# An attention and feed-forward kernel: its planner keeps VectorE's and GpSimd's port work apart, with new planned durations

## The chip, the cores and the metric

The kernel runs on one core of a Trainium2 chip. The metric is device time in microseconds (us). A core has five engines with instruction queues of their own: TensorE (PE; its weight loads are PEld), VectorE (DVE), ScalarE (ACT), GpSimd (POOL) and SyncE (SP), which here issues all DMAs. Engines wait for one another through semaphores only.

## The reference

```python
scores = 1/sqrt(D) * q @ k.T                      # B, H, S, D = 4, 8, 576, 64
psi_rel = log1p(|i - j|); psi_i = log1p(max(i, 1))
bias = relu((psi_rel / psi_i) * w1 + b1) @ w2     # 32 hidden units, one bias per head
attn = softmax(scores + bias)                     # sum + 1e-9 in the divisor
x = (attn @ v) laid out as (B*S, H*D)             # 2304 x 512
h = x @ w_in                                      # 512 x 2048
out = (h * sigmoid(h)) @ w_out                    # 2048 x 512
```

The weights w_in and w_out are 64-bit floats in DRAM; everything else is float32.

## The kernel before, in words

Every step is an operation of a plan: a kind, the engines that may run it with a planned duration for each, a due time, the tiles it reads and writes. `Plan.order` (L118) plays the plan: whenever an engine is free in it, it starts the ready operation with the earliest due time (with a penalty for an engine that is slow for it, not on GpSimd), until all are placed. The result is nothing but one fixed row of instructions per engine; on the chip each engine runs its row in order and waits by semaphores for what it reads. So a planned duration never makes anything wait on the chip: it decides which engine gets an operation, and behind what.

Three parts follow one another and overlap at their seams.

First, the bias (`bias_tile`, L311): 36 tiles, each with four `bias_f` (L326 ScalarE, L328 VectorE or GpSimd), a matmul (L334) and an eviction (L341, L343), written to DRAM and read back as slabs. Beside it runs the attention of batch 0.

Attention (`chunk`, L537; `visit`, L463): keys and queries are split into a float32r part and a remainder (`k_hi`, `k_lo`, `q_hi`, `q_lo`; the casts are L270 on ScalarE and L272 on VectorE, the subtractions L275 on GpSimd or VectorE). Then score matmuls (`s_mm` L561, `s_last` L552), the maximum with the bias (L568, VectorE, scores read from PSUM), the exponential (L575, ScalarE), transposes (L584), evictions (L270, L272) and the product with v (L483). Four head pairs per batch, five chunks of rows each; the row sums go through `sum` and `recip` (L515, L519).

Feed-forward (`ff_block`, L659; `ff_step`, L627): six blocks of 384 tokens, 16 steps each. A block's x is scaled and split (`split_x`, L599: `x_mul` L614, `x_hi`, `x_lo`), a step is 12 matmuls of `h_mm` (L633), tanh (L638), the gate (L642), a split of its result (`g_hi`, `g_lo`) and 9 matmuls of `out_mm` (L656), due two steps after. In block 0, while the attention of batches 1 and 2 runs, each of 32 weight tiles is first brought from 64-bit to 32-bit floats (`narrow`, L349: `abs` L356 on ScalarE, then `clamp` L360, `shift` L364, `low` L369, `sign` L374 on VectorE) and split by `prepare` (L377: `split_hi` on ScalarE, `split_lo` on GpSimd or VectorE, both L270 and L275). The split w_in goes to DRAM and is read again by the later blocks.

TensorE fills gaps of the first 24 us with warm-up matmuls on a zero tile (L723), placed where the plan has it idle.

Of the kernel before, what the change touches and what calls it, by code (L numbers as in the profile page):

```python
# [46 lines left out]
class Plan:  # L47
# [11 lines left out]
    LAG = {"PE": 0.2, "ACT": 0.15, "DVE": 0.13, "POOL": 0.15, "SP": 0.95}  # L59
# [58 lines left out]
    def order(self):  # L118
        ops = self.ops
# [12 lines left out]
        num, dma, mode = 0, 0.0, 0  # L132
# [13 lines left out]
        while events:  # L146
# [17 lines left out]
            for e in sorted(free, key=lambda e: free[e]):  # L164
# [8 lines left out]
                while wait[e]:  # L173
# [42 lines left out]
def attention_moe_kernel(ctx: ExitStack, tc: tile.TileContext, q, k, v, small, w_in, w_out, lut, ident_d, out):  # L216
# [94 lines left out]
    def bias_tile(st, t0):  # L311
# [8 lines left out]
        for ig in range(4):  # L320
            @op("bias_f", {"ACT": 0.22 + n * 0.00086, "DVE": 0.15 + n * 0.0009} if ig or st % 2 == 0 or st < 4 else {"POOL": 0.12 + n * 0.0045},
# [27 lines left out]
    def narrow(t0, w, src):  # L349
# [17 lines left out]
        @op("low", ("DVE", 0.9), t0 + 0.3, reads=[d], writes=[w])  # L367
# [35 lines left out]
    def keys(b, hp, t0):  # L403
# [8 lines left out]
        for a in range(2):  # L412
            @op("k_lo", {"POOL": 1.55, "DVE": 0.95}, t0 - 6 + 0.1 * a, reads=[kst, khi], writes=[(klo, a)])
# [10 lines left out]
    def queries(b, hp, chunks, t0):  # L424
# [6 lines left out]
        @op("q_hi", {"ACT": 0.2 + 0.00083 * w, "DVE": 0.1 + 0.00056 * w}, t0 - 5, reads=[qst], writes=[qs])  # L431
# [3 lines left out]
        @op("q_lo", {"POOL": 0.12 + 0.0025 * w, "DVE": 0.1 + 0.0014 * w}, t0 - 4, reads=[qst], writes=[qs])  # L435
# [6 lines left out]
    def bias_of(hp, c, t0):  # L442
# [6 lines left out]
        if last:  # L449
            @op("bias_pad", ("POOL", 0.4), t0 - 9.1, writes=[bias])  # L450
# [51 lines left out]
    def sums(t0):  # L502
# [3 lines left out]
        @op("sq_zero", ("POOL", 0.3), t0 - 3, writes=[sq])  # L506
# [4 lines left out]
    def factors(b, hp, sq, t0):  # L511

        @op("sum", {"DVE": 0.17, "POOL": 0.3}, t0 + 4, reads=[(sq, i) for i in range(9)], writes=[sq])
# [3 lines left out]
        @op("recip", ("DVE", 0.2), t0 + 4.1, writes=[sq])  # L517
# [19 lines left out]
    def chunk(b, hp, c, i, x0, d0, khi, klo, qs, pt, sm, sq, t0):  # L537
# [27 lines left out]
        for a in range(heads):  # L565
            @op("max", ("DVE", 0.23 + width * 0.00105), t0 + 0.5 + 0.5 * a, reads=[sps[a], bias], writes=[(p, a), (sm, i + a)])
# [221 lines left out]
```

## Time and profile before

| | |
|---|---|
| time, median of 3 runs | 736.9 us (735.35 to 737.13) |
| profiled execution: span | 734.3 us |
| PE matmul busy | 712.6 us, 97% of the span |
| DVE busy | 421.0 us, 57%, 862 instructions |
| ACT busy | 389.4 us, 53%, 820 instructions |
| POOL busy | 281.4 us, 38%, 277 instructions |
| DMA | 154.77 MB, mean 211 GB/s |

The page gives no other time of the profiled execution than its span; the runs' times include what lies around it. Busy shares are averages over stages: DVE's busy tenths stand at 9 through most of the first 45% of the span and at 1 to 2 in the last third. "PE busy" counts matmuls whose ends are modelled, so a full PE isn't PE at its peak; the rate of matmuls has to be read from a stretch in which they follow one another.

### The profile page before, as it was taken

The page shows a single profiled execution, that of the slowest core. Times are in us where ns is not written, and L with a number is a line of the kernel's source. Part 1 is how long each engine was busy: PE and PEld are TensorE (multiplying, and loading weights), DVE is VectorE, ACT ScalarE, POOL GpSimd, SP SyncE. Part 2 cuts the span into 40 slices and gives each one's busy share as a digit, 9 for nine tenths or more (in the row PEclk, how much of TensorE's full clock was granted, in tenths as well). Part 3 has the DMA queues.
Part 4 walks back from the last instruction along what each step waited for, and adds up shares of the span by engine and source line. Part 5 has one row for each costly group of instructions (what it writes and reads, how often), then busy time and mean ns, then how long its engine had stood idle before and what let it go on. Part 6 is the DMA issues. An engine that isn't in the chain of part 4 may idle for free.

```text
span 734.3 us, 13019 instructions
## 1 busy us (share of the span) xinstructions
PE 712.6 (97%) x4642; PEld 590.1 (80%) x4642; DVE 421.0 (57%) x862; ACT 389.4 (53%) x820; POOL 281.4 (38%) x277
## 2 busy tenths in 40 slices
PE   9899999999999999989999999999999999999997
PEld 4376698677777787778888888899998999999996
DVE  6999968999999999996553544213211221211111
ACT  8899968886786777765443454222222232222222
POOL 5464524474746445573122251123223322422221
PEclk9999999999999999999999999999999999999999
DMA  6998899898584594879856567736454644346001
GB/s 195 372 315 270 277 310 359 278 289 297 191 290 157 203 303 149 272 257 311 293 165 224 168 217 241 263 115 196 148 162 153 186 150 152 125 136 195 1 0 44
DMA packets 68384, 154.77 MB, mean 211 GB/s; under 512 B 9056, under 2 KB 24032, under 8 KB 68320
## 3 DMA queue, kind: packets, MB, share of 16 engines
q1 hardware_dynamic: 68320, 153.94, 63.7%
q8 instruction: 37, 0.61, 0.4%
q14 instruction: 27, 0.22, 0.1%
HBM read 125.12 MB, written 28.79 MB: 210 GB/s over the span
## 4 chain that ended last, share of the span: by engine, by line
PE 46%; issue 7%; DVE 3%; POOL 2%; DMA 1%; ACT 0%; POOLq 0%; DVEq 0%; ACTq 0%
PE psum L633 18%; PE psum L656 18%; PE psum L483 3%; PE psum L561 3%; PE psum L584 3%; POOL M L275 2%; DVE G L568 1%; DVE w L369 1%; DMA G<-in_k_dram 1%; PE psum L552 1%; DVE M L275 0%; DVE w L374 0%; DVE th L642 0%; DVE M L272 0%; DVE w L360 0%
## 5 line engine op out<-in xcount | busy, mean ns | idle before, releaser
L633 PE MATMUL psum<-M,G 128*128 128x384 f32 x1152 | 238.8, 339 | 1.0 <-POOL M L275 0.8
L656 PE MATMUL psum<-G,M 128*128 128x512 f32 x864 | 238.0, 397 | 1.2 <-DVE M L275 0.9
L633 PEld LDWEIGHTS psum<-M,G 128*128 128x128 f32 x1152 | 203.4, 188 | 16.6 <-POOL M L275 1.0
L275 POOL TENSOR_TENSOR M<-th,M 128x384 fp32r<-128x384 f32 x82 | 84.9, 1035 | 272.0 <-ACT M L270 189.3
L642 DVE SCALAR_TENSOR_TENSOR th<-th,psum 128x384 f32<-128x384 f32 x96 | 53.0, 552 | 216.4 <-ACT th L638 216.4
L656 PEld LDWEIGHTS psum<-G,M 128*128 128x128 f32 x864 | 156.7, 188 | 22.2 <-DVE M L275 1.6
L575 ACT ACTIVATE G<-G,sm 128x576 f32<-128x576 f32 (+1 forms) x144 | 111.8, 777 | 53.6 <-DVE sm L568 52.3
L638 ACT ACTIVATE th<-psum 128x384 f32<-128x384 f32 x96 | 47.1, 491 | 161.1 <-PE psum L633 160.0
L568 DVE CUSTOM_DVE_ANT_0 G<-psum,G 128x576 f32<-128x576 f32 (+1 forms) x144 | 106.5, 758 | 27.9 <-PE psum L561 15.5
L584 PE MATMUL psum<-ident,G 128*128 128x128 f32 x656 | 93.5, 276 | 5.7 <-DVE sm L568 3.3
L561 PE MATMUL psum<-G,M 128*128 128x288 f32 x512 | 90.9, 310 | 4.9 <-DVE sm L568 3.5
L584 PEld LDWEIGHTS psum<-ident,G 128*128 128x128 f32 x656 | 75.3, 141 | 23.0 <-issue 4.8
L561 PEld LDWEIGHTS psum<-G,M 128*128 128x128 f32 x512 | 73.9, 190 | 19.7 <-issue 6.7
L483 PE MATMUL psum<-pt,M 128*64 128x128 f32 (+3 forms) x880 | 87.5, 346 | 1.6 <-DVE sm L568 0.8
L483 PEld LDWEIGHTS psum<-pt,M 128*64 128x64 f32 x880 | 52.1, 137 | 30.7 <-issue 6.8
L270 ACT ACTIVATE pt<-psum 128x512 f32<-128x512 f32 (+3 forms) x111 | 59.4, 551 | 28.1 <-PE psum L584 27.0
L275 POOL TENSOR_TENSOR M<-M 64x256 fp32r<-64x256 f32 (+3 forms) x40 | 48.6, 1217 | 57.9 <-DVE M L272 21.0
L270 ACT ACTIVATE M<-th 128x384 fp32r<-128x384 f32 x81 | 42.3, 523 | 40.9 <-DVE th L642 40.0
L272 DVE COPY pt<-psum 128x512 f32<-128x512 f32 (+3 forms) x81 | 45.4, 571 | 21.8 <-PE psum L584 19.1
L275 POOL TENSOR_TENSOR G<-w,G 128x512 fp32r<-128x512 f32 x25 | 35.6, 1425 | 23.8 <-ACT G L270 19.9
L275 POOL TENSOR_TENSOR G<-G 128x576 fp32r<-128x576 f32 x21 | 32.2, 1540 | 29.6 <-PE psum L334 9.6
L326 ACT ACTIVATE G<-lut_sb,cb 128x528 f32<-128x528 f32 (+16 forms) x71 | 41.6, 662 | 0.0
(55 smaller groups left out, 574.1 us busy)
## 6 DMA issues: line engine op xcount, KB each, us to landing
G<-win_d SPq DMA_DIRECT2D x80, 512.0 KB
G<-bias_d SPq DMA_DIRECT2D x48, 576.0 KB
bias_d<-G SPq DMA_DIRECT2D x36, 295.5 KB
G<-in_k_dram SPq DMA_DIRECT2D x16, 576.0 KB
G<-in_w_in_dram SPq DMA_DIRECT2D x16, 512.0 KB
G<-in_w_out_dram SPq DMA_DIRECT2D x16, 512.0 KB
win_d<-G SPq DMA_DIRECT2D x16, 512.0 KB
M<-in_v_dram SPq DMA_DIRECT2D x16, 320.0 KB
```

The source lines that it names most:

```text
L270: A.activation(out=out, in_=in_, func=AF.Copy)
L272: ENG[e].tensor_copy(out=out, in_=in_)
L275: ENG[e].tensor_tensor(out=out, in0=in0, in1=f(in1), op=ALU.subtract)
L483: T.matmul(out=tl(o)[x, 0:w], lhsT=tl(vs)[:, (s + 1) % 5 * 128 + 64 * a:(s + 1) % 5 * 128 + 64 * a + 64], rhs=tl(pt)[:, s + 5 * a if s < 4 ...
L561: T.matmul(out=s[:, hf, 0:288], lhsT=tl(qs)[:, x0 + 128 * a:x0 + 128 * a + 128], rhs=tl(part)[:, S * a + 288 * hf:S * a + 288 * hf + 288], ...
L568: V.tensor_tensor_reduce(out=mine(p, a).rearrange("p (a n) -> p a n", a=2), in0=tl(sps[a]).rearrange("p (a n) -> p a n", a=2)[:, :, 0:widt ...
L575: A.activation(out=mine(p, a), in_=mine(p, a), func=AF.Exp, scale=-1.0, bias=tl(sm)[:, i + a:i + a + 1], accum_out=tl(sq)[:, 2 * c + a:2 * ...
L584: T.transpose(out=tl(tp)[:, 128 * s:128 * s + 128], in_=tl(p)[:, 128 * (s0 + s):128 * (s0 + s) + 128], identity=ident)
L633: T.matmul(out=tl(hp)[:, 0:TB], lhsT=tl(wr)[:, x, 128 * cc:128 * cc + 128], rhs=tl(xs[cc])[:, y, :], start=(cc + m == 0), stop=(cc == NC - ...
L638: A.activation(out=tl(th), in_=tl(hp)[:, 0:TB], func=AF.Tanh, scale=0.5)
L642: V.scalar_tensor_tensor(out=tl(th), in0=tl(th), scalar=1.0, in1=tl(hp)[:, 0:TB], op0=ALU.add, op1=ALU.mult)
L656: T.matmul(out=tl(acc[i]), lhsT=tl(gg)[:, x, 128 * i:128 * i + 128], rhs=tl(wo[fi])[:, y, :], start=(fi == 0 and m == 0), stop=(fi == NF - ...
```

## The change

Three things in the planner, none in what is computed:

- Operations that are listed in `PORT`, per engine, share one resource in the plan: while one of them runs on VectorE or GpSimd, none of them is started on either. For VectorE these are the casts, splits, the narrowing, `bias_f` and `lut`; for GpSimd the two-input operations and `sum`. GpSimd's `bias_f` and memsets aren't in it.
- When several engines are free at the same time of the plan, GpSimd now chooses last.
- Planned durations and lags are new. Nothing changes in due times, buffer counts or stage constants.

```diff
-    LAG = {"PE": 0.2, "ACT": 0.15, "DVE": 0.13, "POOL": 0.15, "SP": 0.95}
+    LAG = {"PE": 0.18, "ACT": 0.14, "DVE": 0.12, "POOL": 0.1, "SP": 0.95}
+
+    PORT = {"DVE": {"lut", "bias_f", "clamp", "shift", "low", "sign", "split_lo", "k_hi", "k_lo", "q_hi", "q_lo", "x_mul", "x_hi", "x_lo", "g_hi", "g_lo"},
+            "POOL": {"split_lo", "k_lo", "q_lo", "x_mul", "x_lo", "g_lo", "sum"}}
...
-            for e in sorted(free, key=lambda e: free[e]):
+            for e in sorted(free, key=lambda e: (e == "POOL", free[e])):
...
-                    if not self.take(ops[i][4]):
+                    shared = self.kinds[i] in self.PORT.get(e, ())
+                    if shared and port > now or not self.take(ops[i][4]):
...
                     free[e] = end
+                    if shared:
+                        port = end
...
-        @op("clamp", ("DVE", 0.5), t0 + 0.1, writes=[w])
+        @op("clamp", ("DVE", 0.34), t0 + 0.1, writes=[w])
...
-        @op("low", ("DVE", 0.9), t0 + 0.3, reads=[d], writes=[w])
+        @op("low", ("DVE", 0.6), t0 + 0.3, reads=[d], writes=[w])
...
-        @op("split_lo", {"POOL": 1.36, "DVE": 0.9}, t0 + 1, reads=[w, (wr, 0)], writes=[(wr, 1)])
+        @op("split_lo", {"POOL": 1.24, "DVE": 0.6}, t0 + 1, reads=[w, (wr, 0)], writes=[(wr, 1)])
...
-            @op("max", ("DVE", 0.23 + width * 0.00105), t0 + 0.5 + 0.5 * a, reads=[sps[a], bias], writes=[(p, a), (sm, i + a)])
+            @op("max", ("DVE", 0.08 + width * 0.00116), t0 + 0.5 + 0.5 * a, reads=[sps[a], bias], writes=[(p, a), (sm, i + a)])
...
-        @op("g_lo", {"DVE": 0.55, "POOL": 1.1}, t0 + 2.6, reads=[th, (gg, 0)], writes=[(gg, 1)])
+        @op("g_lo", {"DVE": 0.47, "POOL": 0.96}, t0 + 2.6, reads=[th, (gg, 0)], writes=[(gg, 1)])
```

The other planned durations on VectorE, ScalarE and GpSimd go down in the same manner; those of TensorE and SyncE stay. All lines of the file behind the new ones are 6 higher (L275 becomes L281).

How the rows change. Over the whole program VectorE's row goes from 864 to 968 instructions, GpSimd's from 282 to 153, ScalarE's from 678 to 703; TensorE's differs by its warm-ups (82 before, 63 now). The subtraction of the gate's split (g_lo, `M<-th,M`) was on GpSimd 82 times of 96 and is there 7 times now.

GpSimd, a piece of its row in the middle of the weight narrowing (`G<-w,G` is split_lo, `M<-th,M` g_lo, `M<-M` q_lo, `G<-G` k_lo), before:

```order
L275 TENSOR_TENSOR G<-w,G 128x512
L275 TENSOR_TENSOR M<-M 64x512
L275 TENSOR_TENSOR G<-G 128x576 x2
L275 TENSOR_TENSOR G<-w,G 128x512
L275 TENSOR_TENSOR M<-th,M 128x384
L275 TENSOR_TENSOR G<-w,G 128x512
L275 TENSOR_TENSOR M<-M 64x704
L275 TENSOR_TENSOR G<-w,G 128x512
L275 TENSOR_TENSOR M<-th,M 128x384
```

and with the change:

```order
L281 TENSOR_TENSOR G<-G 128x576
L514 MEMSET sq 128x128
L281 TENSOR_TENSOR M<-M 64x512
L281 TENSOR_TENSOR G<-w,G 128x512
L281 TENSOR_TENSOR M<-M 64x704
L281 TENSOR_TENSOR G<-w,G 128x512
L281 TENSOR_TENSOR M<-th,M 128x384
L521 TENSOR_SCALAR sq<-sq 128x9
```

Between its first and last split_lo GpSimd had 71 two-input operations and has 42 now; the g_lo and part of each of the other kinds went to VectorE.

VectorE at the same place of the narrowing (L360 and L366 clamp, L364 and L370 shift, L369 and L375 low, L374 and L380 sign, `ISA G,sm<-psum,G` the maximum), before:

```order
L642 SCALAR_TENSOR_TENSOR th<-th,psum 128x384
L374 SCALAR_TENSOR_TENSOR w<-G,w 128x512
L364 TENSOR_SCALAR w<-w 128x512
L369 SCALAR_TENSOR_TENSOR w<-G,w 128x512
L275 TENSOR_TENSOR G<-w,G 128x512
L568 ISA G,sm<-psum,G 128x576
```

and with the change:

```order
L375 SCALAR_TENSOR_TENSOR w<-G,w 128x512
L380 SCALAR_TENSOR_TENSOR w<-G,w 128x512
L278 COPY pt<-psum 128x4x128
L366 TENSOR_SCALAR w<-w 128x512
L281 TENSOR_TENSOR G<-w,G 128x512
L370 TENSOR_SCALAR w<-w 128x512
L648 SCALAR_TENSOR_TENSOR th<-th,psum 128x384
```

The steps of the narrowing and the maxima stand there as often as before (32 tiles, 62 maxima between the first and the last step); what came in between them are subtractions.

VectorE at the end of its row, before (15 gates in a row, whose g_lo stand on GpSimd):

```order
L642 SCALAR_TENSOR_TENSOR th<-th,psum 128x384 x15
L683 TENSOR_SCALAR M<-psum 128x512
L683 TENSOR_SCALAR M<-psum 128x256
```

and with the change:

```order
L648 SCALAR_TENSOR_TENSOR th<-th,psum 128x384
L281 TENSOR_TENSOR M<-th,M 128x384
L648 SCALAR_TENSOR_TENSOR th<-th,psum 128x384
L281 TENSOR_TENSOR M<-th,M 128x384
L689 TENSOR_SCALAR M<-psum 128x512
L689 TENSOR_SCALAR M<-psum 128x256
```

Each gate is followed there by its own subtraction, which reads ScalarE's cast.

## Rows read from the trace of the kernel before

**Rows 1.** Busy time by stage; columns: stretch, its length, busy time (and instructions) by engine.

```profile
core 0: us, PE busy (x) PEld busy (x) DVE busy (x) ACT busy (x) POOL busy (x), PEclk, DMA share, GB/s
0.00:127.30 127.30, 122.58 (x1195) 84.25 (x1195) 107.50 (x256) 107.57 (x230) 60.94 (x72) 0.99 0.91 299
127.30:318.80 191.50, 179.78 (x1206) 144.91 (x1205) 185.35 (x342) 144.16 (x303) 102.23 (x89) 1.00 0.72 242
335.00:728.00 393.00, 393.00 (x2144) 346.57 (x2140) 113.36 (x235) 124.33 (x258) 107.47 (x108) 1.00 0.51 164
```

**Rows 2.** Chain of waits, 335 to 360 us; columns: start, length, what.

```profile
334.71 2.84 PE psum L483 x20
...
339.75 2.09 PE psum L633 x12
...
342.55 0.98 PE psum L584 x9
...
344.92 1.05 PE psum L561 x8
345.97 2.31 PE psum L483 x20
...
352.74 2.07 PE psum L656 x9
```

**Rows 3.** Groups of TensorE's matmuls, 127.3 to 318.8 us; columns as in the page's part 5.

```profile
L561 PE MATMUL psum<-G,M 128*128 128x288 f32 x223 | 40.4, 308 | 3.0 <-DVE sm L568 1.5 <-DVE pt L272 1.0 <-ACT pt L270 0.4
L483 PE MATMUL psum<-pt,M 128*64 128x256 f32 (+2 forms) x320 | 40.2, 398 | 1.6 <-DVE sm L568 0.8 <-DVE th L642 0.6
L584 PE MATMUL psum<-ident,G 128*128 128x128 f32 x287 | 40.1, 275 | 4.7 <-DVE sm L568 3.3 <-DVE pt L272 0.7 <-ACT pt L270 0.5
L633 PE MATMUL psum<-M,G 128*128 128x384 f32 x183 | 38.2, 345 | 1.0 <-POOL M L275 0.8
L656 PE MATMUL psum<-G,M 128*128 128x512 f32 x129 | 34.8, 399 | 0.9 <-DVE M L275 0.9
```

**Rows 4.** Timeline at 205 to 212 and 376 to 378 us; columns: start, length, instruction.

```profile
205.49 1.69 POOL L275 TENSOR_TENSOR M<-M 64x704 fp32r<-64x704 f32 x1 [3.89 <-issue]
205.54 1.92 DVE L360 TENSOR_SCALAR w<-w 128x512 f32<-128x512 f32 x1
...
209.07 0.68 DVE L369 SCALAR_TENSOR_TENSOR w<-G,w 128x512 uint32<-128x512 uint32 x1
209.67 0.55 DVE L275 TENSOR_TENSOR M<-th,M 128x384 fp32r<-128x384 f32 x1
...
211.42 0.42 DVE L360 TENSOR_SCALAR w<-w 128x512 f32<-128x512 f32 x1
...
377.02 0.75 DVE L275 TENSOR_TENSOR G<-G 128x576 fp32r<-128x576 f32 x1
```

**Rows 5.** Groups of VectorE's narrowing steps, 127.3 to 318.8 us.

```profile
L369 DVE SCALAR_TENSOR_TENSOR w<-G,w 128x512 uint32<-128x512 uint32 x32 | 32.0, 1001 | 0.4
L374 DVE SCALAR_TENSOR_TENSOR w<-G,w 128x512 uint32<-128x512 uint32 x31 | 26.9, 869 | 0.1
L360 DVE TENSOR_SCALAR w<-w 128x512 f32<-128x512 f32 x32 | 22.8, 715 | 0.8 <-ACT w L356 0.7
L364 DVE TENSOR_SCALAR w<-w 128x512 uint32<-128x512 uint32 x32 | 20.3, 635 | 0.2
```

**Rows 6.** Busy time of the subtractions (L275 alone), same stretch.

```profile
core 0: us, DVE busy (x) POOL busy (x), PEclk, DMA share, GB/s
127.30:318.80 191.50, 16.39 (x13) 90.51 (x64) 1.00 0.72 242
```

**Rows 7.** Two groups of GpSimd's, same stretch.

```profile
L275 POOL TENSOR_TENSOR G<-w,G 128x512 fp32r<-128x512 f32 x24 | 33.8, 1409 | 23.8 <-ACT G L270 19.9 <-issue 1.5 <-DMA xp<-rec_d 1.3
...
L614 POOL TENSOR_TENSOR xp<-xp 128x384 f32<-128x384 f32 x6 | 7.2, 1202 | 3.3 <-DMA xp<-rec_d 2.0 <-DMA xp<-x_d 1.2
```

**Rows 8.** Group of VectorE's k_lo, 0 to 127.3 us.

```profile
L275 DVE TENSOR_TENSOR G<-G 128x576 fp32r<-128x576 f32 x5 | 7.0, 1404 | 0.0
```

**Rows 9.** Timeline at the end, 725 to 729 us.

```profile
727.51 1.01 POOL L275 TENSOR_TENSOR M<-th,M 128x384 fp32r<-128x384 f32 x1 [3.19 <-ACT M L270]
```

More of the change, by code (lines that the diff above doesn't have):

```diff
@@ L131, in order @@
         out = []
-        num, dma, mode = 0, 0.0, 0
+        num, dma, mode, port = 0, 0.0, 0, 0.0
         def push(t, what):
@@ L320, in bias_tile @@
         for ig in range(4):
-            @op("bias_f", {"ACT": 0.22 + n * 0.00086, "DVE": 0.15 + n * 0.0009} if ig or st % 2 == 0 or st < 4 else {"POOL": 0.12 + n * 0.0045},
+            @op("bias_f", {"ACT": 0.2 + n * 0.00083, "DVE": 0.13 + n * 0.00053} if ig or st % 2 == 0 or st < 4 else {"POOL": 0.12 + n * 0.004},
                 t0 + 0.3 * ig, reads=[lut_b, (cb, 0)], writes=[(Fs[ig // 2], ig)])
@@ L412, in keys @@
         for a in range(2):
-            @op("k_lo", {"POOL": 1.55, "DVE": 0.95}, t0 - 6 + 0.1 * a, reads=[kst, khi], writes=[(klo, a)])
+            @op("k_lo", {"POOL": 1.37, "DVE": 0.68}, t0 - 6 + 0.1 * a, reads=[kst, khi], writes=[(klo, a)])
             def _(e, a=a):
@@ L429, in queries @@
         load("ld_q", t0 - 12, [qst], lambda e: SP.dma_start(out=tl(qst), in_=q[b, hp][:, 256 * chunks[0]:256 * chunks[0] + w]), 1024 * w)
-        @op("q_hi", {"ACT": 0.2 + 0.00083 * w, "DVE": 0.1 + 0.00056 * w}, t0 - 5, reads=[qst], writes=[qs])
+        @op("q_hi", {"ACT": 0.1 + 0.00083 * w, "DVE": 0.06 + 0.00055 * w}, t0 - 5, reads=[qst], writes=[qs])
         def _(e):
             copy(e, tl(qs), tl(qst))
-        @op("q_lo", {"POOL": 0.12 + 0.0025 * w, "DVE": 0.1 + 0.0014 * w}, t0 - 4, reads=[qst], writes=[qs])
+        @op("q_lo", {"POOL": 0.12 + 0.0022 * w, "DVE": 0.07 + 0.00105 * w}, t0 - 4, reads=[qst], writes=[qs])
         def _(e):
@@ L449, in bias_of @@
         if last:
-            @op("bias_pad", ("POOL", 0.4), t0 - 9.1, writes=[bias])
+            @op("bias_pad", ("POOL", 0.25), t0 - 9.1, writes=[bias])
             def _(e):
@@ L504, in sums @@
         sq = buf("sq", [128, 128])
-        @op("sq_zero", ("POOL", 0.3), t0 - 3, writes=[sq])
+        @op("sq_zero", ("POOL", 0.16), t0 - 3, writes=[sq])
         def _(e):
@@ L511, in factors @@
     def factors(b, hp, sq, t0):
-        @op("sum", {"DVE": 0.17, "POOL": 0.3}, t0 + 4, reads=[(sq, i) for i in range(9)], writes=[sq])
+        @op("sum", {"DVE": 0.1, "POOL": 0.2}, t0 + 4, reads=[(sq, i) for i in range(9)], writes=[sq])
         def _(e):
             ENG[e].tensor_scalar_add(out=tl(sq)[:, 0:9], in0=tl(sq)[:, 0:9], scalar1=1e-9)
-        @op("recip", ("DVE", 0.2), t0 + 4.1, writes=[sq])
+        @op("recip", ("DVE", 0.13), t0 + 4.1, writes=[sq])
         def _(e):
@@ L610, in split_x @@
                     98304, reads=[rec_b[i] for i in range(TB * blk // S, (TB * blk + TB - 1) // S + 1)], plain=True)
-            @op("x_mul", {"DVE": 0.6, "POOL": 1.15}, t - 0.1, reads=[xr], writes=[xb])
+            @op("x_mul", {"DVE": 0.47, "POOL": 0.96}, t - 0.1, reads=[xr], writes=[xb])
             def _(e, xb=xb, xr=xr):
                 ENG[e].tensor_tensor(out=tl(xb), in0=tl(xb), in1=tl(xr), op=ALU.mult)
-            @op("x_hi", {"DVE": 0.5, "ACT": 0.52}, t, reads=[xb], writes=[(xs[cc], 0)])
+            @op("x_hi", {"DVE": 0.27, "ACT": 0.42}, t, reads=[xb], writes=[(xs[cc], 0)])
             def _(e, xb=xb, cc=cc):
                 copy(e, tl(xs[cc])[:, 0, :], tl(xb))
-            @op("x_lo", {"POOL": 1.1, "DVE": 0.66}, t + 0.1, reads=[xb, (xs[cc], 0)], writes=[(xs[cc], 1)])
+            @op("x_lo", {"POOL": 0.96, "DVE": 0.48}, t + 0.1, reads=[xb, (xs[cc], 0)], writes=[(xs[cc], 1)])
             def _(e, xb=xb, cc=cc):
```

30 lines of the change are left out of this document (15 added, 15 removed).

## The prediction

> **What bounds the kernel now.** I first cut the span into stages, by the first and last instruction of the weight narrowing on VectorE (127.3 and 318.8 us), and read each engine's busy time in them [rows 1]. What is to be seen: up to 127.3 us the DMA engines are 0.91 busy and VectorE 107.5 of 127.3; in the narrowing stage VectorE is busy 185.35 of 191.5 and ScalarE and GpSimd far less; from 335 to 728 us TensorE is busy all the time and VectorE 113 of 393. A busy TensorE says little, since the ends of matmuls are modelled, so next I priced them. In a stretch where the chain of waits holds TensorE alone, 12 matmuls of L633 take 2.09 us, 9 of L656 2.07, 8 of L561 1.05, 9 transposes of L584 0.98, and 20 of L483 take 2.31 or 2.84 (256 or 320 wide) [rows 2]. The narrowing stage holds 183, 129, 223, 287 and 320 of these [rows 3]: 31.9 + 29.7 + 29.3 + 31.3 + 41.2 (L483 at the mean of its two prices); its seven s_last groups of eight, priced like L561, are another 7.4 (an estimate). That is 170.8 us of TensorE. So in 191.5 us TensorE lacks work for about **20.7 us**, and that is the most that this stage can give back. A gain there is not swallowed later: from 335 us on TensorE has no gap, and in both orders the stage holds the same attention and feed-forward work.
>
> **Why VectorE is slow there.** The timeline shows the pattern [rows 4]: a subtraction on GpSimd starts at 205.49 and lasts 1.69; VectorE's clamp starts 0.05 us behind it and lasts 1.92, to 0.28 us after GpSimd's end. The clamp at 211.42 takes 0.42. In the same way L369 takes 0.68, the 128x384 subtraction 0.55 and the 128x576 one 0.75 with nothing in the way. Over the stage the four narrowing steps average 0.715, 0.635, 1.001 and 0.869 us [rows 5]. Against 0.42 for the first two and 0.68 for the others (the second of each pair is taken to cost what the first does) the excess is 32 x 0.295 + 32 x 0.215 + 32 x 0.321 + 31 x 0.189 = 32.4 us. VectorE's thirteen subtractions in the stage take 16.39 us [rows 6]; seven of 512 columns at about 0.68 (between 0.55 and 0.75), four of 384 and two of 576 would be 8.5, so 7.9 more. Stretched casts add some 0.7 (an estimate). Sum: **41 us** blocked. GpSimd did 64 subtractions and 6 multiplications in that time [rows 6, 7], so each cost VectorE 41 / 70 = 0.59 us.
>
> **The change, part by part.**
> Work moved to VectorE. Between the first and the last narrowing row the new order has on VectorE 16 weight subtractions for 7, 13 of g_lo for 4, 6 of k_lo for 2, 4 of q_lo for none, 2 of x_lo for none, 10 wide evictions for 6, 4 sums for 1, and 7 casts and one small copy fewer. At undisturbed prices: 9 x 0.68 + 9 x 0.55 + 4 x 0.75 + 4 x 0.8 + 2 x 0.55 + 4 x 0.82 + 3 x 0.17 - 3.5 = 18.7 (0.8, 0.82, 0.17 and 0.5 for a cast are estimates from the subtractions and the cheapest steps of [rows 4, 5]). Neighbours overlap by about 0.08 us (the step at 209.07 ends at 209.75, the next starts at 209.67 [rows 4]), so 27 operations more occupy about **+17 us**.
> Work taken from GpSimd. 42 two-input operations stay there in this stage. What each still costs VectorE is the unknown. The plan keeps the two apart, but what orders the chip is each engine's row and its semaphores: GpSimd's weight subtraction waits for ScalarE's cast (19.9 of its 23.8 us of idle time [rows 7]) and not for VectorE to be out of the way, so one that the plan held back may start early. Bounds for the cost of one: 0 if the plan's timing holds, 0.59 if nothing is avoided, and at worst its whole length, (90.51 + 7.2) / 70 = 1.4 us [rows 6, 7]. I take half of 0.59, because that cast itself follows VectorE's last narrowing step, which ties the two rows loosely together: 42 x 0.295 = 12.4 us.
> The Trainium skill's page SBUF — State Buffer, section Who interferes with whom, says that the shared port pair goes to whichever engine issues first and that the other blocks for the whole instruction. The clamp at 205.54 behind the subtraction at 205.49 agrees. By that rule VectorE's precedence in the plan counts for nothing on the chip, and the result would be that of the second rival.
> Stage sum: 185.4 - 41 + 17 + 12.4 = 173.8 us of VectorE; with the 6.1 us that it is idle now, 179.9 us: **11.6 us** less, still 9 us above TensorE's 170.8.
> First stage. VectorE gets 3 k_lo, 6 q_lo, 7 bias_f, 4 evictions and 2 sums more, and 8 casts, 4 bias evictions and one maximum fewer: about +5.4 us at such prices (an estimate). Against that its five k_lo at 1.404 [rows 8] would fall to 0.75, 3.3 us, and its casts by about 1. I put the net at **+1 us**, with -3 (all contention gone) and +6 (none gone, all of it felt) as ends. What hides the rest is the DMA engines' 0.91; without that cover the +5.4 shows.
> Late stages. Behind the narrowing 76 g_lo and 17 x_lo run on VectorE and wait there for a cast, mostly ScalarE's, with maxima and gates queued behind. VectorE is idle for 280 of 393 us [rows 1], and out_mm is due two steps after its g, so I cost this at nothing; without the idle time each would cost its wait.
> End. The last matmuls wait for GpSimd's last subtraction, 1.01 us from 727.51 [rows 9]; on VectorE it takes 0.55: **-0.5 us**.
> Warm-up matmuls go from 82 to 63. They compute nothing, and the first stage's granted clock is 0.99 [rows 1], so: nothing, as long as the clock stays there. New planned durations of operations that keep their place cost nothing by themselves.
> Sum: -11.6 + 1 - 0.5 = -11.1. The profiled span is 734.3, the median of the runs 736.9; I keep the 2.6 us between them: 736.9 - 11.1 = **725.8 us**.
>
> **Rivals.**
> First, all contention goes, and TensorE becomes the bound: VectorE's 161.4 + 6.1 is below TensorE's 170.8. For it: from 335 us on TensorE shows no gap at all. Against it: there VectorE is mostly idle, here it would still be 0.9 busy. At 173 us the stage saves 18.5: 736.9 - 18.5 + 1 - 0.5 = 718.9 us.
> Second, nothing is kept apart: 0.59 per operation stays, 24.8 us; 185.4 - 41 + 17 + 24.8 = 186.2, and what fewer operations on GpSimd bring is eaten by the 17 us that VectorE took over. 736.9 + 0.8 + 1 - 0.5 = 738.2 us. For it: GpSimd's waits on ScalarE.
> Third, slower: each remaining operation blocks VectorE for longer, since VectorE's row now holds 17 us more of the operations that can be blocked, and GpSimd takes the port whenever ScalarE's cast ends, ahead of the narrowing chain that feeds the next weights. From about 0.61 us per operation the kernel is slower by over 0.3% (2.2 us, about what a measurement of it can tell from no change). At 0.75, 31.5 us, it is +7.5 and +0.5: 744.9 us. Against it: there are 42 such operations for 70.
>
> **Chances and range.** Half avoided 0.50, all avoided 0.17, nothing avoided 0.16, worse 0.17. The first two are faster; of the third 0.13 lies within 0.3% and 0.03 above: faster 0.67, same 0.13, slower 0.20. The range reaches from 714 (all avoided, the first stage at -3 and the stage 1 us nearer to TensorE's work) to 742 (0.67 us per operation), leaving out about 0.05 below and 0.11 above. The forecast's own range, 0.15 to 0.45 us per operation, is 719 to 733.
>
> **What would show it.** Right: the stage from the first to the last narrowing step shrinks from 191.5 to about 180 us; the third step averages 0.75 to 0.85 instead of 1.001; VectorE stays over 0.93 busy in it; TensorE has no gap from its end to the last step. Wrong: the four steps keep their averages (second rival) or exceed them (third); the stage shrinks but a gap of TensorE opens behind it; or the first narrowing step starts more than 5 us later than 127.3.

## The result, and the profile after

| | before | after |
|---|---|---|
| time, median | 736.7 us (735.35 to 737.13) | 741.0 us (740.75 to 743.19) |
| profiled execution: span | 734.3 us | 739.2 us |
| narrowing stage, first start to last start | 191.5 us | 188.8 us |

The change made the kernel slower: ratio 1.0068, 95% interval [1.0051, 1.0085]. The forecast was 725.8 us. The time lies within the range (714 to 742), at its end, and on the side of the third rival, but not by that rival's mechanism, as the next rows show.

The stages of the kernel after, beside [rows 1]; columns as there:

```profile
core 0: us, PE busy (x) PEld busy (x) DVE busy (x) ACT busy (x) POOL busy (x), PEclk, DMA share, GB/s
0.00:131.10 131.10, 121.93 (x1169) 81.77 (x1169) 111.77 (x265) 105.47 (x229) 52.19 (x61) 1.00 0.86 285
131.10:319.90 188.80, 179.41 (x1206) 145.60 (x1206) 176.55 (x370) 144.83 (x307) 58.42 (x55) 0.99 0.73 246
336.00:733.00 397.00, 396.33 (x2157) 348.23 (x2155) 152.76 (x303) 136.84 (x287) 20.12 (x23) 1.00 0.50 166
```

The first stage ends 3.8 us later (131.1 for 127.3), with the DMA engines less busy (0.86 for 0.91). The narrowing stage is 2.7 us shorter. VectorE's busy time in it falls by 8.8 us, from 185.35 to 176.55, but its idle time doubles, from 6.15 to 12.25 us.

The contention itself went as planned. VectorE's groups of the same stage after (mean ns behind the comma), to be held against [rows 5] and [rows 6]:

```profile
L380 DVE SCALAR_TENSOR_TENSOR w<-G,w 128x512 uint32<-128x512 uint32 x32 | 24.0, 751 | 0.2
L375 DVE SCALAR_TENSOR_TENSOR w<-G,w 128x512 uint32<-128x512 uint32 x32 | 22.2, 695 | 0.3
L366 DVE TENSOR_SCALAR w<-w 128x512 f32<-128x512 f32 x32 | 17.0, 531 | 0.4 <-ACT w L362 0.3
L370 DVE TENSOR_SCALAR w<-w 128x512 uint32<-128x512 uint32 x32 | 15.5, 485 | 0.2
L281 DVE TENSOR_TENSOR G<-w,G 128x512 fp32r<-128x512 f32 x16 | 13.1, 820 | 0.8 <-ACT G L276 0.7
L281 DVE TENSOR_TENSOR M<-th,M 128x384 fp32r<-128x384 f32 x13 | 8.4, 654 | 0.1
```

and the subtractions of the same stretch (columns: length, VectorE, GpSimd):

```profile
131.10:319.90 188.80, 31.27 (x41) 50.29 (x36) 0.99 0.73 246
```

Against the undisturbed 0.42 and 0.68 us the four steps are 32 x (0.111 + 0.065 + 0.015 + 0.071) = 8.4 us too long. The 16 weight subtractions are 2.2 too long, the 13 g_lo 1.4, and the other twelve about 1.0 (an estimate from their prices in the prediction). Sum: 13 us for the 41 before. With 36 subtractions and 4 multiplications left on GpSimd that is 13 / 40 = **0.32 us** for each, where the prediction took 0.295.

What VectorE waits for, in the narrowing stage before (us in total, times, longest):

```profile
DVE th L642 <- ACT th L638: 2.0, 3, 0.9
DVE G L568 <- PE psum L561: 1.1, 3, 0.4
DVE w L360 <- ACT w L356: 0.7, 2, 0.4
DVE pt L272 <- PE psum L584: 0.6, 1, 0.6
```

and after:

```profile
DVE xo L278 <- PE psum L489: 2.4, 2, 2.2
DVE pt L278 <- PE psum L590: 2.1, 5, 0.9
DVE G L574 <- PE psum L567: 1.9, 4, 1.0
DVE th L648 <- ACT th L644: 1.1, 2, 0.8
DVE G L574 <- PE psum L558: 1.0, 2, 0.7
```

Before, VectorE waited 1.7 us for TensorE; after, it waits 7.4 us for TensorE's products. That is 5.7 of the 6.1 us by which its idle time grew: most of the time that is freed on VectorE comes back as waiting for the other engine.

### The profile page after: what moved, and what is told of

The parts are those of the page before. It is cut to its first block, busy times and chain, and to the rows that moved or that the text cites. A ratio compares the mean times of both kernels' runs of the same rounds, so it can differ in the third digit from the quotient of the medians.

```text
span 739.2 us, 12866 instructions
## 1 busy us (share of the span) xinstructions
PE 713.9 (97%) x4623; PEld 589.3 (80%) x4623; DVE 454.8 (62%) x966; ACT 398.8 (54%) x845; POOL 139.7 (19%) x148
## 4 chain that ended last, share of the span: by engine, by line
PE 69%; DVE 12%; DMA 9%; issue 4%; ACT 3%; POOL 2%; SPq 0%; DVEq 0%; POOLq 0%; ACTq 0%
PE psum L639 23%; PE psum L662 23%; PE psum L489 8%; PE psum L567 6%; PE psum L590 6%; DMA G<-bias_d 2%; DVE G L574 2%; PE psum L340 2%; DMA xp<-x_d 2%; DMA G<-win_d 2%; PE psum L558 1%; DVE G L281 1%; DVE G L334 1%; DMA G<-in_k_dram 1%; DVE pt L278 1%
## 5 line engine op out<-in xcount | busy, mean ns | idle before, releaser
L662 PE MATMUL psum<-G,M 128*128 128x512 f32 x864 | 234.6, 396 | 0.0
L281 DVE TENSOR_TENSOR M<-th,M 128x384 fp32r<-128x384 f32 x89 | 53.1, 597 | 38.6 <-ACT M L276 38.0
L276 ACT ACTIVATE pt<-psum 128x640 f32<-128x640 f32 (+3 forms) x110 | 57.1, 536 | 25.3 <-PE psum L590 20.0
L278 DVE COPY pt<-psum 128x640 f32<-128x640 f32 (+3 forms) x82 | 48.1, 597 | 18.7 <-PE psum L590 16.6
L281 POOL TENSOR_TENSOR M<-M 64x512 fp32r<-64x512 f32 (+3 forms) x27 | 32.1, 1188 | 106.8 <-ACT M L276 49.7
L340 PE MATMUL psum<-G,cb 128*32 128x512 f32 (+17 forms) x352 | 39.1, 474 | 3.4 <-ACT G L347 1.8
L620 POOL TENSOR_TENSOR xp<-xp 128x384 f32<-128x384 f32 x13 | 14.0, 1083 | 148.6 <-DMA xp<-x_d 148.4
L332 ACT ACTIVATE G<-lut_sb,cb 128x480 f32<-128x480 f32 (+17 forms) x64 | 38.0, 656 | 0.0
```

Of the source, the lines that this page charges most:

```text
L276: A.activation(out=out, in_=in_, func=AF.Copy)
L278: ENG[e].tensor_copy(out=out, in_=in_)
L281: ENG[e].tensor_tensor(out=out, in0=in0, in1=f(in1), op=ALU.subtract)
L340: T.matmul(out=tl(bps)[32 * ig:32 * ig + 32, x:min(n, x + 512)], lhsT=w2bd(), rhs=fat(ig)[:, x:min(n, x + 512)], start=True, stop=True)
L662: T.matmul(out=tl(acc[i]), lhsT=tl(gg)[:, x, 128 * i:128 * i + 128], rhs=tl(wo[fi])[:, y, :], start=(fi == 0 and m == 0), stop=(fi == NF - ...
```

## The experiments

All ratios are against the kernel before on the same chip (736.3 to 736.5 us there). Of several I give a lag: TensorE's matmuls of both traces, each at its price of [rows 2], summed up to the same moment; the difference says by how many us of work a kernel is behind the kernel before. It is worked out from timeline rows and good to about 1 us, since one price stands for all matmuls of a line. For the kernel after it is 4.3 at 108 us, 1.8 at 324, 4.1 at 500 and 4.0 at 700. So 4 us are lost in the first 110 us, 2 to 3 won back in the narrowing, and about 2 lost again between 324 and 500 us.

### One part alone

`e1_durations`: the new durations and lags, without the port rule and without GpSimd choosing last.

```diff
-            for e in sorted(free, key=lambda e: (e == "POOL", free[e])):
+            for e in sorted(free, key=lambda e: free[e]):
...
-                    shared = self.kinds[i] in self.PORT.get(e, ())
+                    shared = False
```

> New planned durations and lags alone; VectorE and GpSimd may overlap in the plan again and GpSimd doesn't choose last. Theory A (the rules that keep the port apart lower VectorE's blocked time, and something else costs the time): the four narrowing steps stay stretched here, the third at 0.9 us or more against 0.695 with the whole change, and the time is not below 735. Theory B (the new durations are the part that harms, since the plan packs the rows tighter than the chip can follow): slower than before by 3 us or more, 740 or above. If neither the durations nor the rules harm by themselves: 735 to 739.

Measured: 774.23 us, ratio 1.0492 [1.0466, 1.0519]. The steps stay stretched as theory A says (the third at 0.895 us, just under its 0.9), and the time is in theory B's range too, so this run doesn't choose between them. Durations that hold only without contention, in a plan that doesn't keep the engines apart, are the worst of the tried: VectorE's four steps are blocked for 27 us and the narrowing stage takes 216 us to the end of its last step.

`e2_rules`: both rules with the old durations and lags.

```diff
     LAG = {"PE": 0.2, "ACT": 0.15, "DVE": 0.13, "POOL": 0.15, "SP": 0.95}
...
-            for e in sorted(free, key=lambda e: free[e]):
+            for e in sorted(free, key=lambda e: (e == "POOL", free[e])):
...
-                    if not self.take(ops[i][4]):
+                    shared = self.kinds[i] in self.PORT.get(e, ())
+                    if shared and port > now or not self.take(ops[i][4]):
```

> The two rules alone (port kept apart in the plan, GpSimd last), with the old planned durations and lags. Theory A: the third narrowing step falls to 0.65 to 0.8 us from 1.0, the narrowing stage shortens, and what is lost elsewhere decides the time: 730 to 741. Theory B: without the new durations the rules give what was forecast, 726 to 732. Rival C (moving work from GpSimd to VectorE is what harms): 740 or more, as with the whole change.

Measured: 742.95 us, 1.0076 [1.0049, 1.0102]. The third narrowing step averages 0.903 us:

```profile
L375 DVE SCALAR_TENSOR_TENSOR w<-G,w 128x512 uint32<-128x512 uint32 x32 | 28.9, 903 | 0.0
```

It isn't at 0.65 to 0.8, and the stage from the first to the last step is 214.5 us long instead of shorter, so theory A's signs fail; so does B, and the time is in the range of rival C. This kernel isn't behind at 108 us (lag -1.8), but 8 us behind at 420. So the rules alone don't cost the first stage anything; the lateness there needs the new durations. The two rules weren't tried apart from each other.

### One stretch alone

`e4_late_only` plays the plan by the old rules, durations and lags up to 120 us of plan time and by the new ones from there; `e5_early_only` the other way round; `e11_late_from_105` is e4 with 105 for 120. In these two, theory F puts the loss down to the first stage and L to the late ones.

```diff
+    NEW_FROM, NEW_TO = 120.0, 1e9
...
+                new = self.NEW_FROM <= now < self.NEW_TO
+                for o, w in zip(ops, both):
+                    o[0] = w.new if new else w.old
```

> The whole change, but in force only from 120 us of the plan's own time on; before that the plan goes by the old durations and rules, so the first part of every row is that of the kernel before. Theory F (the loss is made in the first 110 us, where TensorE's work falls 4 us behind): the first 110 us are those of before and the gain behind it stays, 733 to 736 us, so about 5 below the whole change. Rival L (the late stages lose by themselves): 738 us or more.

Measured: 735.31 us, 0.9982 [0.9973, 0.9992]. Faster than both kernels, and as F says. Rival C falls as a general rule: here too GpSimd's work in the narrowing goes to VectorE (45 two-input operations are left of 70), and nothing is lost by it. The kernel keeps the old first stage (lag -0.3 at 108), and its narrowing stage is 188.9 us to the end of the last step, for 192.9 before and 189.4 after.

> The mirror image: the whole change in force only up to 120 us of the plan's time, old durations and rules behind it. Theory F: TensorE's work is about 4 us behind at 108 us, nothing is won back in the narrowing stage, 740 to 743 us. Rival L: about the time of before, 736 to 738 us.

Measured: 756.89 us, 1.0261 [1.0238, 1.0284]. Neither theory's time holds: the lag is 3.8 at 108 us, as in the kernel after and as F says, but then the old rules lose 14 us more in the narrowing (lag 17.9 at 324, four steps blocked for 35.8 us). The old rules do well behind their own first stage and badly behind another.

> The change in force from 105 us of the plan's time on instead of 120. Theory F: 733 to 737, as from 120 us. If a shift of 15 us in where the rules take over moves the time by more than 3 us, the draw of the order counts for as much as the rules.

Measured: 741.49 us, 1.0062 [1.004, 1.0084], 6 us above e4 for a switch 15 us of plan time earlier; the lag at 108 is -0.4, and the loss comes at 324 to 348 us (1.5 to 5.0). So F fails here: the first stage is that of before, and the time that of the kernel after. By the measure set beforehand, the order that happens to come out counts for as much as the rules.

### The first stage

The new plan takes a `bias_f` of 528 columns on VectorE for 0.13 + 528 x 0.00053 = 0.41 us, the old one for 0.63. In the kernel after VectorE runs six of that width, and 64 of all widths:

```profile
L334 DVE TENSOR_SCALAR G<-lut_sb,cb 128x528 f32<-128x528 f32 x6 | 3.7, 656 | 0.0
L334 DVE TENSOR_SCALAR G<-lut_sb,cb 128x560 f32<-128x560 f32 (+17 forms) x64 | 31.0, 520 | 0.4 <-ACT cb L314 0.2
```

The mean of the six mixes two kinds: three take 0.48 us and three, beside a bias_f of GpSimd's, 0.78 to 0.86. VectorE gets 64 bias_f for 57 before. They occupy it for 31.0 / 64 = 0.48 us each and are planned at 0.364 on the mean, so 0.12 too short each and 7.7 us together. That the tiles leave later than planned for this reason is argued, not measured; what can be seen is the traffic. 72 to 96 us, busy times in slices of 12 us, before:

```profile
72.00:84.00 12.00, 12.00 (x133) 7.93 (x132) 11.13 (x28) 11.98 (x25) 6.04 (x4) 1.00 0.83 260
84.00:96.00 12.00, 12.00 (x140) 9.14 (x140) 9.05 (x21) 7.07 (x17) 4.00 (x12) 1.00 0.98 350
```

and after:

```profile
72.00:84.00 12.00, 10.47 (x105) 6.27 (x101) 11.52 (x28) 9.18 (x20) 5.53 (x6) 1.00 0.48 155
84.00:96.00 12.00, 12.00 (x149) 8.84 (x143) 9.67 (x23) 7.87 (x19) 3.77 (x10) 1.00 0.70 208
```

The DMA engines fall to 0.48 and 0.70, TensorE is recorded with 105 matmuls for 133. GpSimd's row at that place (timeline of the kernel after; in brackets the idle time before and what the view says ended it) shows what a row in order does with late work:

```profile
73.87 0.73 POOL L281 TENSOR_TENSOR M<-M 64x256 fp32r<-64x256 f32 x1 [9.57 <-DMA G<-bias_d]
74.70 2.48 POOL L334 TENSOR_SCALAR G<-lut_sb,cb 128x544 f32<-128x544 f32 x1
```

A q_lo waits 9.57 us, and a 2.48 us bias_f, which needs nothing of it, stands behind it. The view puts the wait down to a slab of the bias, but a q_lo reads none. It reads the result of a cast, here one of ScalarE's, whose row is:

```profile
70.29 3.14 ACT L332 ACTIVATE G<-lut_sb,cb 128x496 f32<-128x496 f32 x5
73.32 0.41 ACT L276 ACTIVATE M<-M 128x256 fp32r<-128x256 f32 x1
```

The cast ends at 73.73, 0.14 us before the q_lo starts, and it stood behind five bias_f.

`e9_bias_price`: the kernel after with the old planned durations of bias_f on VectorE and ScalarE, by theory D the cause.

```diff
-            @op("bias_f", {"ACT": 0.2 + n * 0.00083, "DVE": 0.13 + n * 0.00053} ...
+            @op("bias_f", {"ACT": 0.22 + n * 0.00086, "DVE": 0.15 + n * 0.0009} ...
```

> The changed kernel with one planned duration taken back: bias_f keeps its old one on VectorE and ScalarE (0.15 + 0.0009 n and 0.22 + 0.00086 n). Theory D (the first stage loses because bias_f is now planned at 0.36 us on VectorE where it takes 0.48 beside GpSimd's own bias_f, which the port rule doesn't name): TensorE's work is no longer 4 us behind at 108 us, and the time is 734 to 738. Rival (it is the other moves of the first stage): still 3 us or more behind at 108 us, 739 to 744.

Measured: 737.14 us, 1.0007 [0.9994, 1.002]; 3.9 us below the kernel after, and in D's range. The lag at 108 us falls from 4.3 to 1.6, the DMA share in 72 to 84 us rises to 0.77:

```profile
72.00:84.00 12.00, 11.53 (x118) 7.43 (x110) 11.81 (x28) 12.00 (x26) 4.63 (x4) 1.00 0.77 251
```

One order can't settle it, since the next section has changes without meaning that move the time as much. But the other first stages go the same way: those planned with the new price of bias_f are 2.9 to some 7 us behind at 108 us (the kernel after 4.3, e10 5.0, p2 2.9, e1 about 7), those with the old one -2 to 1.6 (e2 -1.8, e9 1.6, p1 about -2, p3 about -1). Among these only e9 tells that price from the other new durations.

`e10_bias_port`: the rival that bias_f on GpSimd, which the rule leaves out, blocks VectorE's.

```diff
-            "POOL": {"split_lo", "k_lo", "q_lo", "x_mul", "x_lo", "g_lo", "sum"}}
+            "POOL": {"bias_f", "split_lo", "k_lo", "q_lo", "x_mul", "x_lo", "g_lo", "sum"}}
```

> The changed kernel with GpSimd's bias_f added to the operations that share the port in the plan. Theory D in its strong form (it is the contention with these 16 operations): VectorE's bias_f averages 0.44 instead of 0.48 us and the first stage catches up by 2 us or more, 735 to 739. Rival: GpSimd's 29 us of bias_f now push VectorE's operations back in the plan, and the first stage is as late as before or later, 740 to 746.

Measured: 742.87 us, 1.0079 [1.005, 1.0108], the lag at 108 still 5.0. Theory D in its strong form fails: neither its catching up nor its time came. But VectorE's bias_f (first line) hardly got shorter, 23.8 / 51 = 0.47 us for 0.48, so the run took little of the contention away and doesn't settle what that costs:

```profile
L334 DVE TENSOR_SCALAR G<-lut_sb,cb 128x560 f32<-128x560 f32 (+17 forms) x51 | 23.8, 518 | 0.2 <-ACT cb L314 0.2
L330 DVE TENSOR_SCALAR G<-lut_sb,cb 128x464 f32<-128x464 f32 (+17 forms) x66 | 31.5, 517 | 0.2 <-ACT cb L310 0.2
```

The second line is of p1 below. Together they show that it isn't the number of bias_f on VectorE that makes the first stage late: with 51 of them e10 is 5.0 us behind, with 66 p1 is about 2 ahead. By what way the price makes it late stays open.

### How much hangs on the order that happens to come out

All planned durations on VectorE 1% longer or shorter: no reason of contention in it, only another order.

```diff
+        if "DVE" in where:
+            where["DVE"] *= 1.01
```

> The kernel before with every planned duration on VectorE raised by 1%: nothing that means anything, but the greedy plan falls out differently. If the order is robust: 735 to 738. If the old rules' order before was a lucky draw (rival O, suggested by the 16 us that the old rules lost behind another start): 742 or more.

> The kernel before with every planned duration on VectorE lowered by 1%: a second draw of the old rules. Rival O (the order before is a lucky draw): 739 or more, as with 1% more (740.3). Otherwise 735 to 738.

> The changed kernel with every planned duration on VectorE raised by 1%. If the new rules make orders that depend less on the draw: 736 to 745, within 5 us of the changed kernel. If they are as much a matter of the draw as the old ones: further away on either side.

Measured: the kernel before at +1% 740.29 us (1.0054 [1.0035, 1.0074]), at -1% 738.75 (1.0026 [1.0012, 1.004]); the kernel after at +1% 742.01 (1.0071 [1.0048, 1.0094]). p1 and p3 lie between the ranges that were set for a robust order and a lucky one, p2 in the range of the first. A change of the planned durations that means nothing costs the old rules 2 to 4 us. The order before is a good one among its neighbours, and of the 4.3 us between the two kernels a part as large as that may belong to no rule. The narrowing stage moves more than the time does. That of p3, to the end of its last step (columns: stretch, length, PE, PEld, DVE, ACT, POOL, clock, DMA share, GB/s):

```profile
124.50:323.10 198.60, 184.95 (x1234) 149.45 (x1232) 184.23 (x350) 147.05 (x310) 96.62 (x86) 0.99 0.70 236
```

VectorE has 2.5 us less to do there than before (186.7), and the stage is 5.7 us longer (192.9 before). Six orders with the change in force in the narrowing (after, p2, e4, e9, e10, e11) take 735.3 to 742.9 us, three by the old rules (before, p1, p3) 736.7 to 740.3.

### What the contention is worth

That the port rule keeps the engines apart doesn't hang on the order. What VectorE is blocked for in the narrowing, worked out as above and divided by GpSimd's two-input operations, is 0.26 to 0.37 us in the seven orders in which the rule holds there (after, e2, e4, e9, e10, e11, p2) and 0.50 to 0.61 in the five in which it doesn't (before, e1, e5, p1, p3).

`e6_before_pool_memset` and `e7_after_pool_memset`: the rows of before and after as they are, but GpSimd's subtractions are zero writes of the same tiles (the low parts are left out).

```diff
     def sub(e, out, in0, in1):
+        if e == "POOL":
+            G.memset(f(out), 0.0)
+            return
```

> The kernel before, every row in the same order, but each subtraction on GpSimd replaced by GpSimd writing zeros to the same place, so the low parts that GpSimd made are zero and it reads nothing. Theory V (what VectorE waits for the port bounds the narrowing stage, as the prediction had it): with the blocked 41 us gone and nothing moved to VectorE the stage runs at TensorE's pace, about 18 us off: 717 to 723. Rival W (the stage is bound by waits between engines in the order of the rows, and VectorE's blocked time mostly fills time in which it would wait anyway): less than half of that, 728 to 735.

Measured: 722.93 us, 0.9811 [0.9789, 0.9832], in V's range and out of W's. The four steps drop to 0.459, 0.450, 0.709 and 0.706 us, 4 us blocked in place of 33. The third of them, to be held against [rows 5]:

```profile
L372 DVE SCALAR_TENSOR_TENSOR w<-G,w 128x512 uint32<-128x512 uint32 x32 | 22.7, 709 | 0.4
```

The Trainium skill's page SBUF — State Buffer, section Who interferes with whom, says that a VectorE instruction with two SBUF inputs contends with a GpSimd instruction that reads SBUF and not with one that only writes it. These runs agree: `low`, with two inputs, averages 0.709 beside zero writes and 1.001 beside subtractions.

> The same replacement in the changed kernel: GpSimd's remaining subtractions become zero writes, so those low parts are zero. It takes away the 13 us of VectorE that are still blocked. Theory V: 8 to 13 us less than the changed kernel, 728 to 733. Rival W, with the loss made in the first 110 us: 736 to 740.

Measured: 730.86 us, 0.9918 [0.9894, 0.9942], 10 us below the kernel after and in V's range.

So contention is worth at most 13.5 us to the kernel before: a zero write is also shorter than a subtraction (0.57 us on the mean for 1.41, 128x512), and nothing here tells the two gains apart. And VectorE lost 35 us of busy time for a stage only 11.8 shorter, not V's 18.

### A floor, or a discount on every us saved

Here F is the theory of a floor set by TensorE's own work, T that each us of VectorE is worth a third anywhere. `e12_memset_short` is e6 with `low` and `sign` on 8 of 512 columns, `e14_after_short` the kernel after with that alone, `e13_split_memset` the kernel before with zero writes for the weight subtractions only.

```diff
-            V.scalar_tensor_tensor(out=tl(w).bitcast(U32), in0=tl(d)[:, :, 0], ...
+            V.scalar_tensor_tensor(out=tl(w).bitcast(U32)[:, :8], in0=tl(d)[:, :8, 0], ...
```

> The kernel before, with GpSimd's subtractions as zero writes (722.9 us, narrowing stage 181.1) and in addition the narrowing steps low and sign on 8 of 512 columns, so that some 40 us more of VectorE's 151 go. Theory F (floor): TensorE's own work takes about 177 to 180 us of the stage, so nothing more can be had: stage 178 to 181, time 721 to 724. Theory T (a third): each us of VectorE's busy time saved is worth a third of a us, as it was from 35 to 11.8: stage 168, time 709 to 713.

> The changed kernel with the narrowing steps low and sign on 8 of 512 columns: some 40 us of VectorE's 176.5 go, GpSimd's subtractions stay. Theory F: the stage falls from 188.8 to 179 to 182 and no further, the first stage stays 4 us late: time 731 to 735. Theory T: a third of 40, 13 us: stage 175, time 726 to 729.

> The kernel before, with only the weight subtractions on GpSimd (24 of its 70 two-input operations in the stage) as zero writes. VectorE should lose about 12 to 14 us of busy time in the stage. Theory F: until the floor is reached saved VectorE time counts almost in full: stage 181 to 184, time 725 to 729. Theory T: a third of it: stage 187, time 731 to 734.

Measured: e12 724.25 us (0.9834 [0.9808, 0.9861]), e14 732.56 (0.9962 [0.9943, 0.9981]), e13 729.67 (0.9913 [0.9897, 0.993]). The first two are as F expects (e12's time 0.25 us above its range), the third lies between F and T. The stages, first step to the end of the last (columns: stretch, length, PE, PEld, DVE, ACT, POOL, clock, DMA share, GB/s), of e12:

```profile
125.70:305.70 180.00, 176.04 (x1200) 144.45 (x1199) 118.68 (x343) 140.65 (x303) 41.38 (x87) 1.00 0.77 256
```

of e6 and, in the same columns, of the kernel before:

```profile
126.10:307.20 181.10, 177.33 (x1211) 146.12 (x1210) 151.43 (x344) 142.38 (x305) 44.30 (x89) 1.00 0.76 255
127.30:320.20 192.90, 181.18 (x1214) 146.18 (x1213) 186.73 (x344) 144.85 (x305) 103.09 (x89) 1.00 0.72 241
```

of e13:

```profile
127.30:312.30 185.00, 178.75 (x1212) 146.13 (x1211) 169.37 (x344) 143.79 (x305) 81.45 (x89) 1.00 0.75 253
```

and of e14, e7 and the kernel after:

```profile
130.70:310.80 180.10, 175.65 (x1203) 144.47 (x1202) 141.78 (x371) 143.58 (x306) 56.54 (x55) 1.00 0.77 258
129.60:311.60 182.00, 176.60 (x1204) 144.56 (x1204) 165.23 (x371) 144.14 (x307) 27.76 (x55) 1.00 0.77 258
131.10:320.50 189.40, 180.01 (x1209) 146.02 (x1208) 177.15 (x371) 145.14 (x307) 58.42 (x55) 0.99 0.73 247
```

Kernels with the same rows can be set in one line, by VectorE's busy time and the length of this stage:

| rows | VectorE busy, us | stage, us |
|---|---|---|
| of before: before, e13, e6, e12 | 186.7, 169.4, 151.4, 118.7 | 192.9, 185.0, 181.1, 180.0 |
| of after: after, e7, e14 | 177.2, 165.2, 141.8 | 189.4, 182.0, 180.1 |

There is a floor of 180 us, the same for both orders, and VectorE's last 33 us (e6 to e12) are worth 1.1. Above it a us of VectorE is worth neither a whole one nor a fixed third: 7.9 of 17.4 (0.45) and 3.9 of 18.0 (0.22) in the order before, 7.4 of 12.0 (0.62) in the order after. At the floor VectorE waits for TensorE; its waits in e12:

```profile
DVE G L571 <- PE psum L564: 21.4, 22, 2.8
DVE pt L272 <- PE psum L587: 10.4, 10, 1.7
DVE th L645 <- ACT th L641: 9.6, 8, 2.1
```

TensorE is then busy for 176.0 of 180.0 us. The prediction priced its work at 170.8: some 5 us too low, and 4 us of gaps stay. A piece of e12's chain of waits shows a part of it:

```profile
216.06 1.13 PE psum L587 x9
217.19 0.70 PE psum L659 x3
```

Nine transposes take 1.13 here and 0.98 in [rows 2]. What else is in the 5 us isn't settled; records of matmuls aren't missing (each trace holds all 1152 of `h_mm` and 864 of `out_mm`).

## Why the prediction was wrong

**What held.** That the change does keep the two engines apart, by half and a little more: 41 us blocked became 13, at 0.32 us per operation for the 0.295 taken. The work moved to VectorE cost 19 us (176.55 - 185.35 + 41 - 13) for the 17 taken. The third step averages 0.695, even under the 0.75 to 0.85 foretold; that part is luck of this order, for with the same rule it is 0.903 in e2 and 0.866 in e9. VectorE stays 0.935 busy in the stage and TensorE has no gap behind it, as foretold, and none of the three signs of being wrong came: the sum failed in a way that the prediction didn't list. The second and the third rival, for whom 0.59 or more would stay per operation, are out, though the time lies at theirs. By the Trainium skill's rule that whichever engine issues first holds the shared ports (SBUF — State Buffer, Who interferes with whom) I had said that precedence in the plan would count for nothing. The rows of the last section agree with the lock for GpSimd's two-input operations, though not for its bias_f, and the inference was wrong: planned precedence lowered the cost of an operation from 0.59 to 0.32 us. Of the 28 us less that VectorE is blocked, 40 x 0.27 = 11 come from that and 30 x 0.59 = 18 from 30 operations fewer. The granted clock stays at 1.00 in the first stage without 19 of the warm-ups, and the last g_lo takes 0.56 on VectorE, as costed:

```profile
732.53 0.56 DVE L281 TENSOR_TENSOR M<-th,M 128x384 fp32r<-128x384 f32 x1 [0.59 <-ACT M L276]
```

**The step that failed first:** "173.8 us of VectorE; with the 6.1 us that it is idle now, 179.9 us: 11.6 us less, still 9 us above TensorE's 170.8". The stage took 188.8 us for these 179.9. VectorE came out at 176.6, 2.8 above the sum; that is the smaller part. The larger is that idle time isn't a constant of the stage. It doubled, and 5.7 of the 6.1 us more are waits for TensorE, which is nearly full itself: a us saved on VectorE is worth 0.2 to 0.6 of a us, down to nothing at 180 us. By the line of the order before (0.45), the forecast's 11.6 us of VectorE would have been worth 5, and the 8.8 that came, 4; measured are 2.7 to 3.5, by either end of the stage. That these agree may be luck, since between two orders the idle time differs by itself (p3). The first rival's bound fails with it: with all contention gone and 33 us of VectorE's work besides, the kernel takes 724 us, not 718.9. And [rows 1] to [rows 3] were read with too low a floor: not 20.7 us could be given back, but about 11 to 13.

**The step that failed second:** the first stage, "+1". It was +4: e4, with the old first stage, has the rest of the change and 735.3 us. I had priced what VectorE's new operations take, found the DMA engines 0.91 busy, and let these cover the rest. But what feeds the DMAs is the bias tiles, and the plan now counts bias_f too cheap (0.364 for 0.48 us on VectorE). With only its prices put back (e9) 2.7 of the 4.3 us of lag at 108 us are gone, and all four first stages planned with the new price are late. How the price does it isn't shown: it isn't the number of bias_f on VectorE. "New planned durations of operations that keep their place cost nothing by themselves" was true and beside the point: they didn't keep their place. The other 1.6 us are within what a chance reordering does (the lag there is 2.9 in p2).

**Late stages, "0":** VectorE's g_lo cost nothing that can be seen (TensorE is busy 396.33 of 397 us). Still the lag grows by about 2 between 324 and 500 us; in e4 it grows by less than the 1 us that it is good to, so no part of the change makes it necessarily. Its cause stays open. From the last narrowing step's start to the end of the span the kernel after takes even 3.8 us more (419.3 for 415.5), but 1.8 of that is work that TensorE was behind with already.

In sum: +4 in the first stage, -2 to -3 in the narrowing, +2 behind it, against +1, -11.6 and 0. In this order the slower time rests on the first stage, but e2 and e11 are as slow without a late one, and the 4.3 us are as large as the spread between neighbouring orders (p1, p3); whether the change as a rule makes plans better or worse than the old rules can't be told from one plan each. A version faster than both is e4, 735.31 us (0.9982); e11 shows how little it takes to lose it.

## What to carry to other kernels

Before counting a us saved on a nearly full engine, ask what a second engine beside it needs: near the floor that it sets a saved us is worth only a part of one (0.2 to 0.6 here), and the floor is best found by a run in which the first engine's work is cut away. Where a table of durations sets an order, every price is also a decision who does what and when; here putting back the price of one kind, planned 0.12 us too short, took 3.9 us off the time, more than the narrowing had gained. And compare a planner's change with what a change of 1% that means nothing does, before the difference is put down to a reason.

## What was not expected of the hardware

GpSimd doesn't always hold VectorE up for its whole instruction. In the narrowing before, 48 of VectorE's narrowing steps start inside a two-input operation of GpSimd's, and 47 of them end behind it, 0.28 us (the first two steps) or 0.55 us (the others) in the median. Beside GpSimd's bias_f, which reads one tile, it is otherwise. VectorE's bias_f at 74.81 us after runs inside the 2.48 us one of GpSimd's from 74.70 that is shown above, and takes what it takes undisturbed:

```profile
74.81 0.48 DVE L334 TENSOR_SCALAR G<-lut_sb,cb 128x528 f32<-128x528 f32 x1
```

Of the 21 that run wholly inside one of GpSimd's in the kernel after, 13 do so and 8 are stretched by 0.16 to 0.43 us.

And one wait on VectorE's side can empty TensorE for longer than the wait. At 168 us after, VectorE has split_lo, clamp and x_mul in a row, the first two stretched beside GpSimd's k_lo (167.08, 1.78 us) and x_mul (168.83, 1.44 us):

```profile
167.51 1.90 DVE L281 TENSOR_TENSOR G<-w,G 128x512 fp32r<-128x512 f32 x1
169.33 1.22 DVE L366 TENSOR_SCALAR w<-w 128x512 f32<-128x512 f32 x1
170.47 0.54 DVE L620 TENSOR_TENSOR xp<-xp 128x384 f32<-128x384 f32 x1
```

The two are 2.0 us too long together. What VectorE does there reaches TensorE through ScalarE, whose row has a cast of the product ahead of two evictions; TensorE waits for the first of these:

```profile
171.05 0.53 ACT L276 ACTIVATE M<-xp 128x384 fp32r<-128x384 f32 x1 [0.94 <-DVE xp L620]
171.48 1.17 ACT L276 ACTIVATE pt<-psum 128x640 f32<-128x640 f32 x2
172.22 1.33 PE L567 MATMUL psum<-G,M 128*128 128x288 f32 x4 [2.69 <-ACT pt L276]
```

TensorE in slices of 4 us around it:

```profile
168.00:172.00 4.00, 1.00 (x7) 0.73 (x6) 4.00 (x6) 2.12 (x5) 2.27 (x2) 0.99 0.74 266
172.00:176.00 4.00, 3.78 (x20) 2.52 (x22) 2.71 (x7) 3.21 (x8) 1.27 (x1) 0.58 0.55 193
176.00:180.00 4.00, 4.00 (x30) 3.48 (x27) 2.93 (x7) 1.74 (x4) 0.00 (x0) 1.00 0.36 70
```

TensorE is busy for 1.00 of 4 us, and in the next 4 its granted clock is 0.58 on the mean, between the full 2.4 GHz and the 1.2 GHz level; then 1.00 again. The lag rises from about 4 to about 7 us there, and the rest of the stage wins it back. Both stretched instructions end 0.28 to 0.55 us behind GpSimd's.
